# A linear-attention and mixture-of-experts kernel: three batches in flight, with four engines in program order

## The chip, the cores and the metric

The kernel runs on one core of one Trainium2 chip. Time is device time in microseconds (us) of one execution, as a median over runs; lower is better. Profiles come from one further execution, taken by the hardware profiler; its span is the time from its first to its last instruction.

The engines are named as in the profile: PE is TensorE (PEld its weight loads), DVE is VectorE, ACT is ScalarE, POOL is GpSimd, SP is SyncE, which here only issues DMA transfers. "Granted clock" is the share of full speed that PE's throttle allowed, as the profile shows it.

## The reference

There are 8 batches of 576 tokens. First comes a linear attention with 8 heads of width 64, and an RMS norm; its result, 512 wide, is the input x of a layer of 4 attention experts (head width 64), of which each token uses two.

```python
kv  = einsum('bhsd,bhse->bhde', k, v)              # 64x64 per head
out = einsum('bhsd,bhde->bhse', q, kv)
x   = out / sqrt(mean(out*out, -1) + 1e-6) * g_norm
...
logits = x @ w_gate                                # 4 experts, the best 2 kept, softmax over them
for e in range(4):
    q, k, v = x @ wq[e], x @ wk[e], x @ wv[e]
    a  = softmax(causal(q @ k.T / 8))
    ye = a @ v @ wo[e]
    result += weight_of_e_for_this_token * ye
```

## The kernel before

The tokens of a batch are cut into five blocks: four of 128 and one of 64. All eight batches pass through the same two stages and an output stage. Each stage is a Python generator: it emits instructions for one piece of work and yields a number, the weight of that piece.

**stage1(b)** (lines 191 to 314) is the linear attention. PE forms kv of each head pair (`kv_pair`, L179, 80 matmul instructions), and `kv_copy` brings it to SBUF twice, by DVE (L187) and by ACT (L188). PE transposes q block by block (`q_block`, L200, copied by DVE at L205), transposes kv (L216) and multiplies it with the gate weights (L224), so that the gate's logits come out of the same product as the attention. Then for each of the five blocks: the product p_out on PE (L243, 8 instructions), a copy o_sb by DVE (L250), the squares sq by ACT (L254), and their sum ms by DVE (L260). When all five are there, DVE computes 1/sqrt(ms) for the whole batch with an integer first guess and four Newton steps of three small operations (L271 to L281), forms the logits (L284, L290), and POOL scales the five blocks to x_tok (L296). PE transposes them (p_x, L307) and ACT copies the result to xT (L312).

**stage2(b)** (lines 317 to 495) is the expert layer. DVE and ACT compute the gate (L322 to L341). PE projects v (p_v, L347, copied by DVE to vext, L354). For each of two pairs of experts: `proj` makes q and k (L365, copied by ACT at L376); `scores` makes the causal scores in five pieces (p_sc, L393), ACT takes exp into PT (L403) and POOL masks the diagonal (L408); `pv` multiplies with v (p_O, L445), and DVE normalizes into osc (L460, L461, L465); `o_t` transposes osc (L477), copied by ACT to OT (L482). The emission order is all of p_v, then proj(0), scores(0), proj(1), scores(1), the output stage of the batch before, pv(0), o_t(0), pv(1), o_t(1).

**final(b)** (lines 497 to 508) is the output stage: p_y on PE (L501), a copy by ACT (L506) and a DMA to the result, five times.

Results of PE go through eight PSUM banks in two pools: three tiles of two banks ("big": p_proj, p_sc, p_O, p_out) and two of one bank ("small": p_kv, p_q, p_kt, p_kg, p_x, p_v, p_OT, p_y). A tile is handed to its next user when its readers are done.

The order in which work is emitted is set by `weave` (lines 519 to 531): for each piece of stage2(b) it advances stage1(b+1), the side stream, until that has reached a target share of its own weights. The side stream reaches the end of its out blocks when stage2 is at 72%, and is let on to the norm and the transposes of x when stage2 is at 92%. So in the loop over b two batches are in flight: stage2 of b and stage1 of b+1. The emitted order is not the order on the engines: the framework's planner orders each engine's instructions by readiness and emission order, with durations of its own, and then sets the semaphores. Loads (`load_qkv`) of batch b+2 are emitted at the start of iteration b; q, k and v have two sets of buffers.

Of the kernel before, what the change touches and what calls it, by code (L numbers as in the profile page):

```python
# [10 lines left out]
FP32R = mybir.dt.float32r  # L11
BF16 = mybir.dt.bfloat16
# [6 lines left out]
def kernel(  # L19
# [45 lines left out]
    def small(shape, name, dtype=FP32):  # L65
        return ps1.tile(shape, dtype, tag="small", name=name)
# [121 lines left out]
            nc.scalar.copy(kv2[pp, :, hh * Dh : (hh + 1) * Dh], p_kv[pp, :, :])  # L188


    def stage1(b, res):
        qb, kb, vb = loads[b]
        qT = s1.tile([P, NCH, S], FP32, tag="qT", name="qT", bufs=1)
        kvb, kv2 = kvx[b % 2], kv2s[b % 2]
# [39 lines left out]
            q_block(i)  # L234
            yield 0.5

        xT = s1.tile([P, NCH, S], FP32R, tag="xT", name="xT")
        lg8, ms = lg8s[b % 2], mss[b % 2]

        for i, (t0, nt) in enumerate(blocks):  # L240
# [33 lines left out]
            out=y[:].bitcast(I32), in0=half[:], scalar1=-1.0, scalar2=float(0x5F3759DF),  # L274
            op0=AluOpType.mult, op1=AluOpType.add,
        )
        for it in range(4):
            u, w, y2 = tiny("u"), tiny("w"), tiny("y")
            nc.vector.scalar_tensor_tensor(out=u[:], in0=y[:], scalar=0.5, in1=y[:], op0=AluOpType.mult, op1=AluOpType.mult)
            nc.vector.tensor_tensor(out=w[:], in0=u[:], in1=m, op=AluOpType.mult)  # L280
            nc.vector.scalar_tensor_tensor(out=y2[:], in0=w[:], scalar=1.5, in1=y[:], op0=AluOpType.subtract, op1=AluOpType.mult)  # L281
            y = y2
        gl = blk.tile([P, NB * H, E], FP32, tag="gl", name="gl")
        nc.vector.tensor_tensor(  # L284
# [9 lines left out]
        for i, (t0, nt) in enumerate(blocks):  # L294
# [5 lines left out]
                op=AluOpType.mult,  # L300
            )
            xts.append(xt)
        yield 0.0
        for i, (t0, nt) in enumerate(blocks):
            p_x = small([P, NCH, P], "p_x")
            for c in range(NCH):
# [7 lines left out]
        res["xT"] = xT  # L314


    def stage2(b, res, prev_y):
        xT = res["xT"]
        lg8 = lg8s[b % 2]
        m8 = moe.tile([P, NB, 8], FP32, tag="m8", name="m8")  # L320
# [20 lines left out]
        nc.vector.tensor_tensor(out=gate[:], in0=gt[:], in1=rden[:].unsqueeze(2).to_broadcast([P, NB, E]), op=AluOpType.mult)  # L341

        vx = vexts[b % 2]
        for i, (t0, nt) in enumerate(blocks):
            p_v = small([P, E * Hd], "p_v")
            for c in range(NCH):
                nc.tensor.matmul(  # L347
                    p_v[:nt, :],
                    lhsT=xT[:, c, t0 : t0 + nt],
                    rhs=w_r["v"][:, c, :, :].rearrange("p e f -> p (e f)"),  # L350
                    start=(c == 0),
                    stop=(c == NCH - 1),
                )
            nc.vector.tensor_copy(  # L354
                out=vx[:nt, i, :, 0:Hd], in_=p_v[:nt].rearrange("p (e f) -> p e f", e=E)
            )
            yield 0.47

        def proj(pr):
            out_t = []  # L360
# [20 lines left out]
            res["qk", pr] = out_t  # L381

        def scores(pr):
            qTp, kTp = res["qk", pr]
            PT = moe.tile([P, 2, strips], BF16, tag="PT", name="PT", bufs=3)
# [38 lines left out]
            piece([(3, 3 * P, S), (4, 4 * P, S)])  # L424
            mask(3)
            mask(4)
            yield 0.2
            res["PT", pr] = PT

        OT = moe.tile([P, EP, S], BF16, tag="OT", name="OT")  # L430

        def pv(pr):
            PT = res["PT", pr]
            p_O = big("p_O")
            inv = moe.tile([P, NB, 2], FP32, tag="inv", name="inv")
            osc = moe.tile([P, NB, 2, Hd], BF16, tag="osc", name="osc")
            groups = ((0, (0, 1, 2)), (1, (3, 4)))
            for bank, qcs in groups:
                for n, qc in enumerate(qcs):
                    s0, nq = blocks[qc]  # L440
                    for el in range(2):
                        for kb in range(qc + 1):
                            nk = blocks[kb][1]
                            col = strip_off[kb] + s0 - kb * P
                            nc.tensor.matmul(  # L445
                                p_O[:nq, bank, (2 * n + el) * (Hd + 1) : (2 * n + el + 1) * (Hd + 1)],
                                lhsT=PT[:nk, el, col : col + nq],
                                rhs=vx[:nk, kb, 2 * pr + el, :],
                                start=(kb == 0),
                                stop=(kb == qc),  # L450
                            )
                    yield 0.11 * (qc + 1)
                for sub in ((qcs,) if bank == 0 else ((3,), (4,))):
                    nq = blocks[sub[0]][1]
                    n0, nn = sub[0] - qcs[0], len(sub)
# [15 lines left out]
            res["osc", pr] = osc  # L471
# [12 lines left out]

        yield from proj(0)
        yield from scores(0)
        yield from proj(1)
        yield from scores(1)
        if prev_y is not None:
            yield from prev_y  # L490
        yield from pv(0)
        yield from o_t(0)
        yield from pv(1)
        yield from o_t(1)
        res["OT"] = OT

    def final(b, OT):
        for qc, (s0, nq) in enumerate(blocks):
            p_y = small([P, D], "p_y")
# [8 lines left out]
            yield 0.45  # L508


    W1, W2 = 14.0, 14.3
    OUT_END = 11.6 / W1

    def target(a):
        if a < 0.92:
            return min(a / 0.72, 1.0) * OUT_END
        return 1.0

    def weave(main, side):
        a = s = 0.0  # L520
        live = side is not None
        for c in main:
            a += c / W2
            while live and s < target(a):
                try:
                    s += next(side) / W1
                except StopIteration:
                    live = False
        if live:
            for _ in side:  # L530
                pass

    res = {}
    for _ in stage1(0, res):
        pass
    y_gen = None
    for b in range(B):
        if b + 2 < B:
            loads[b + 2] = load_qkv(b + 2)
        nxt = {}  # L540
        weave(stage2(b, res, y_gen), stage1(b + 1, nxt) if b + 1 < B else None)
        y_gen = final(b, res["OT"])
        res = nxt
    for _ in y_gen:
        pass


# [28 lines left out]
```

## Time and profile before

| | |
|---|---|
| three timed runs | 361.71, 362.43, 363.38 us; median 362.43 |
| profiled execution | 362.53 us, of which the span is 360.7 |
| mean granted clock of PE | 0.837 |
| PE busy | 291.8 us, 81% of the span, 2616 instructions |
| DVE busy | 188.2 us, 52%, 561 instructions |
| ACT busy | 153.0 us, 42%, 273 instructions |
| POOL busy | 80.4 us, 22%, 148 instructions |
| DMA | 30.42 MB read, 9.44 MB written |

A busy PE isn't PE at its peak: its matmuls are pipelined and their ends are modelled, so a matmul row's duration is longer than the distance to the next start. A rate is better read from the starts of successive groups in the timeline. In the timeline each row has the start, the busy time, the engine, the line, the operation with out<-in, and the count; brackets at the end hold the idle time before it and what ended that. The chain of waits follows the work that ended last back from the end; "issue" in it is time in which the engine waited for nothing that the profile shows.

### The profile page before, as it was taken

What the parts mean: (1) busy time and instruction counts of PE and PEld (TensorE: products, weight loads), DVE (VectorE), ACT (ScalarE), POOL (GpSimd) and SP (SyncE); (2) the same over time, 40 slices, a digit from 0 to 9 for tenths busy, and PEclk for the clock granted to TensorE, in tenths of its full rate; (3) what the DMA queues carried; (4) which work ended last, traced back from release to release, by engine and by line L of the source; (5) the groups of instructions that cost most, each with busy time, mean ns of one, the idle gap of its engine ahead of it and who ended that gap; (6) DMA issues with size and microseconds to landing.
All of it is one profiled execution on the core that took longest, in us unless ns stands there. A gap on an engine that the chain in (4) does not pass through costs nothing.

```text
span 360.7 us, 6721 instructions
## 1 busy us (share of the span) xinstructions
PE 291.8 (81%) x2616; PEld 234.8 (65%) x2624; DVE 188.2 (52%) x561; ACT 153.0 (42%) x273; POOL 80.4 (22%) x148
## 2 busy tenths in 40 slices
PE   2782898849994999949995899949996799949883
PEld 2581687638863788638964698638874598728551
DVE  0259654772458444781558444781458534783040
ACT  0202345432581336622572326722663326713833
POOL 8000602150220502150220502141210502132220
PEclk9997599977997599956998599966998589965966
DMA  7968999901737066600872056700002000300213
GB/s 218 214 167 222 241 266 263 207 16 45 220 89 176 2 207 135 185 0 13 250 177 87 2 159 164 195 11 2 2 37 93 2 2 0 133 1 2 88 45 132
DMA packets 75280, 40.30 MB, mean 112 GB/s; under 512 B 54000, under 2 KB 70384, under 8 KB 75248
## 3 DMA queue, kind: packets, MB, share of 16 engines
q1 hardware_dynamic: 75248, 39.86, 42.6%
q8 instruction: 21, 0.34, 0.4%
q14 instruction: 11, 0.09, 0.1%
HBM read 30.42 MB, written 9.44 MB: 110 GB/s over the span
## 4 chain that ended last, share of the span: by engine, by line
PE 56%; issue 22%; ACT 9%; POOL 5%; DVE 4%; DMA 1%; SPq 1%; DVEq 0%; ACTq 0%; POOLq 0%
PE p_proj L365 11%; PE p_x L307 10%; PE p_v L347 7%; PE p_kv L179 7%; PE p_q L200 5%; PE p_out L243 5%; ACT PT L403 4%; POOL x_tok L296 4%; PE p_sc L393 4%; PE p_kg L224 2%; PE p_y L501 2%; DVE o_sb L250 2%; DMA v_b<-in_v_dram 1%; POOL PT L408 1%; ACT y L506 1%
## 5 line engine op out<-in xcount | busy, mean ns | idle before, releaser
L307 PE MATMUL p_x<-ident_f,x_tok 128*128 128x128 f32 (+1 forms) x160 | 39.2, 411 | 39.2 <-POOL x_tok L296 38.1
L408 POOL TENSOR_SCALAR_AFFINE_SELECT PT<-PT 128x256 bf16<-128x256 bf16 (+1 forms) x80 | 29.9, 383 | 167.8 <-ACT PT L403 167.0
L296 POOL TENSOR_TENSOR x_tok<-o_sb,y 128x512 f32<-128x512 f32 (+1 forms) x40 | 42.1, 1083 | 96.7 <-DVE y L281 96.7
L403 ACT ACTIVATE PT<-p_sc 128x576 bf16<-128x576 f32 (+3 forms) x80 | 53.5, 712 | 17.7 <-PE p_sc L393 17.6
L307 PEld LDWEIGHTS p_x<-ident_f,x_tok 128*128 128x128 f32 (+1 forms) x160 | 26.9, 216 | 48.5 <-POOL x_tok L296 45.3
L243 PE MATMUL p_out<-kvx,qT 128*128 128x136 f32 (+1 forms) x320 | 45.8, 291 | 1.6 <-ACT PT L403 0.6
L243 PEld LDWEIGHTS p_out<-kvx,qT 128*128 128x128 f32 (+1 forms) x320 | 38.9, 182 | 6.3 <-ACT PT L403 3.3
L205 DVE COPY qT<-p_q 128x512 f32<-128x512 f32 (+1 forms) x40 | 24.8, 637 | 27.7 <-PE p_q L200 27.7
L354 DVE CAST vext<-p_v 128x256 bf16<-128x256 f32 (+1 forms) x40 | 17.0, 425 | 39.5 <-PE p_v L347 39.1
L254 ACT ACTIVATE sq<-p_out 128x512 f32<-128x512 f32 (+1 forms) x40 | 23.8, 595 | 27.8 <-DVE o_sb L250 19.2
L250 DVE COPY o_sb<-p_out 128x544 f32<-128x544 f32 (+1 forms) x40 | 28.8, 720 | 12.9 <-PE p_out L243 10.6
L260 DVE TENSOR_REDUCE ms<-sq 128x8 f32<-128x520 f32 (+1 forms) x40 | 27.3, 684 | 12.7 <-ACT sq L254 12.7
L445 PE MATMUL p_O<-vext,PT 128*128 128x65 bf16 (+2 forms) x480 | 29.1, 200 | 4.9 <-DVE osc L465 4.2
L179 PE MATMUL p_kv<-v_b,k_b 128*64 128x64 f32 x512 | 28.1, 275 | 6.0 <-DMA v_b<-in_v_dram 5.9
L445 PEld LDWEIGHTS <-PT 128*128 128x128 bf16 (+2 forms) x480 | 23.2, 103 | 13.8 <-issue 9.7
L179 PEld LDWEIGHTS p_kv<-v_b,k_b 128*64 128x64 f32 x512 | 25.2, 187 | 8.0 <-DMA k_b<-in_k_dram 4.5
L347 PE MATMUL p_v<-wv_r,xT 128*128 128x256 f32 (+1 forms) x160 | 30.4, 329 | 0.0
L312 ACT CAST xT<-p_x 128x512 fp32r<-128x512 f32 (+1 forms) x40 | 21.7, 543 | 18.0 <-PE p_x L307 17.9
L393 PE MATMUL p_sc<-qTp,kT 64*128 64x288 f32 (+2 forms) x192 | 25.0, 338 | 2.3 <-ACT PT L403 1.5
L347 PEld LDWEIGHTS p_v<-wv_r,xT 128*128 128x128 f32 (+1 forms) x160 | 25.0, 215 | 1.8
L365 PE MATMUL p_proj<-xT,wq_r 128*128 128x288 f32 x128 | 25.7, 321 | 0.3 <-ACT PT L403 0.3
L501 PE MATMUL p_y<-wo_b,OT 128*128 128x512 bf16 (+1 forms) x72 | 23.4, 409 | 1.8 <-ACT OT L482 1.4
(67 smaller groups left out, 370.5 us busy)
## 6 DMA issues: line engine op xcount, KB each, us to landing
q_b<-in_q_dram SPq DMA_DIRECT2D x32, 256.0 KB, 4.7
out_dram<-y SPq DMA_DIRECT2D x32, 256.0 KB, 2.0
k_b<-in_k_dram SPq DMA_DIRECT2D x7, 1024.0 KB, 5.8
v_b<-in_v_dram SPq DMA_DIRECT2D x7, 1024.0 KB, 8.6
k_b<-in_k_dram SPq DMA_DIRECT2D x4, 256.0 KB, 4.2
v_b<-in_v_dram SPq DMA_DIRECT2D x4, 256.0 KB, 4.5
k_rem<-in_k_dram SPq DMA_DIRECT2D x8, 128.0 KB, 8.5
v_rem<-in_v_dram SPq DMA_DIRECT2D x8, 128.0 KB, 7.5
```

The costliest lines, as they stand in the source:

```text
L179: nc.tensor.matmul(p_kv[hh * Dh : (hh + 1) * Dh, c, :], lhsT=lk, rhs=rv, start=(j == 0), stop=(j == NF), skip_group_check=True,)
L243: nc.tensor.matmul(p_o[:nt, c // 2, (c % 2) * 2 * GW : (c % 2 + 1) * 2 * GW], lhsT=qT[:, c, t0 : t0 + nt], rhs=kvb[:, c, :, :].rearrange(" ...
L250: nc.vector.tensor_copy(out=ob[:nt, i].rearrange("p (k h) g -> p k (h g)", k=2), in_=p_o[:nt, :, 0 : 4 * GW])
L296: nc.gpsimd.tensor_tensor(out=xt[:nt], in0=ob[:nt, i, :, 0:Dh], in1=y[:nt, i * H : (i + 1) * H].unsqueeze(2).to_broadcast([nt, H, Dh]), op ...
L307: nc.tensor.transpose(p_x[:, c, :nt], xts[i][:nt, 2 * c : 2 * c + 2, :].rearrange("p h d -> p (h d)"), ident_f[:nt, :nt],)
L347: nc.tensor.matmul(p_v[:nt, :], lhsT=xT[:, c, t0 : t0 + nt], rhs=w_r["v"][:, c, :, :].rearrange("p e f -> p (e f)"), start=(c == 0), stop= ...
L365: nc.tensor.matmul(p_p[:, s, 0:HALF], lhsT=w_r[nm][:, c, 2 * pr : 2 * pr + 2, :].rearrange("p e f -> p (e f)"), rhs=xT[:, c, s * HALF : (s ...
L393: nc.tensor.matmul(p_s[:, el, o : o + hi - lo], lhsT=kTp[pb, kb * P : (kb + 1) * P], rhs=qTp[pb, lo:hi], start=True, stop=True,)
L403: nc.scalar.activation(PT[:, :, d0 : d0 + o], p_s[:, :, 0:o], ACTF.Exp, scale=scale)
L408: nc.gpsimd.affine_select(out=d, in_=d, compare_op=AluOpType.is_ge, fill=0.0, base=0, pattern=[[0, 2], [1, w]], channel_multiplier=-1,)
L445: nc.tensor.matmul(p_O[:nq, bank, (2 * n + el) * (Hd + 1) : (2 * n + el + 1) * (Hd + 1)], lhsT=PT[:nk, el, col : col + nq], rhs=vx[:nk, kb ...
L501: nc.tensor.matmul(p_y[:nq, :], lhsT=OT[:, pr, s0 : s0 + nq], rhs=wo_b[:, pr, :], start=(pr == 0), stop=(pr == EP - 1),)
```

## The change

stage1 is cut in two. `stage_a` is stage1 up to x_tok; `stage_x` holds the five transposes p_x and their copies to xT. stage2 becomes `stage_s`. A loop iteration merges three batches: stage_s of b, stage_x of b+1 and stage_a of b+2. Before the loop, stage_a(0) runs alone, and then stage_x(0) beside stage_a(1). Each stream has a start and an end in the iteration (stage_s 0 to 1, stage_x 0.05 to 0.4, stage_a 0.1 to 1.0); `merge` always advances the stream that stands earliest.

All of it is traced under `tc.manual_schedule` with PE, ACT, DVE and POOL named: on these engines the instructions stay in the order in which they are emitted, and the planner doesn't move them. SP's DMA issues are not in the list.

Within stage_s the order is written out as a string of keys: Q0, Q1 the projections, V p_v, S0, S1 the scores, P0, P1 p_O, T0, T1 the transposes of osc, Y the output stage of the batch before. The pieces of `pv` are cut so that the normalization is emitted with the last p_O piece of its group. Loads of batch b+3 are emitted at the start of iteration b.

The norm takes three Newton steps in place of four. Each step's last operation had given (w - 1.5) * y, of the wrong sign, which four steps cancel; `reverse0=True` makes it (1.5 - w) * y.

```diff
-    def stage1(b, res):
+    def stage_a(b, res):
...
-        xT = s1.tile([P, NCH, S], FP32R, tag="xT", name="xT")
...
-        for it in range(4):
+        for it in range(3):
...
-            nc.vector.scalar_tensor_tensor(out=y2[:], in0=w[:], scalar=1.5, in1=y[:], op0=AluOpType.subtract, op1=AluOpType.mult)
+            nc.vector.scalar_tensor_tensor(
+                out=y2[:], in0=w[:], scalar=1.5, in1=y[:], op0=AluOpType.subtract, op1=AluOpType.mult, reverse0=True
+            )
...
-        yield 0.0
+        res["x_tok"] = xts
+
+
+    def stage_x(res):
+        xts = res["x_tok"]
+        xT = s1.tile([P, NCH, S], FP32R, tag="xT", name="xT")
         for i, (t0, nt) in enumerate(blocks):
             p_x = small([P, NCH, P], "p_x")
...
-    def stage2(b, res, prev_y):
+    def stage_s(b, res, prev_y):
...
-                    yield 0.11 * (qc + 1)
+                    if qc != qcs[-1]:
+                        yield 0.11 * (qc + 1)
...
+                yield 0.11 * (qcs[-1] + 1)
...
-        yield from proj(0)
-        yield from scores(0)
-        yield from proj(1)
-        yield from scores(1)
-        if prev_y is not None:
-            yield from prev_y
-        yield from pv(0)
-        yield from o_t(0)
-        yield from pv(1)
-        yield from o_t(1)
-        res["OT"] = OT
-
+        st = {"V": v_proj(), "Q0": proj(0), "Q1": proj(1), "S0": scores(0), "S1": scores(1)}
+        st.update({"P0": pv(0), "P1": pv(1), "T0": o_t(0), "T1": o_t(1), "Y": prev_y})
+        order = (
+            "Q0 Q0 V V S0 V S0 V S0 V S0 Q1 S0 Q1 S1 Y S1 Y S1 P0 P0 P0 S1 P0 P0 S1 Y T0 Y Y P1 P1 P1 P1 P1 T1"
+        )
+        for key in order.split():
+            if st[key] is not None:
+                yield next(st[key])
...
+    def merge(*streams):
+        live = [[t0, t0, (t1 - t0) / cost, gen] for gen, cost, t0, t1 in streams if gen is not None]
+        while live:
+            x = min(live, key=lambda x: x[0])
+            try:
+                x[0] += next(x[3]) * x[2]
+            except StopIteration:
+                live.remove(x)
+
+    CA, CX, CS = 11.8, 2.25, 14.5
+    with tc.manual_schedule(engines={mybir.EngineType.PE, mybir.EngineType.Activation, mybir.EngineType.DVE, mybir.EngineType.Pool}):
+        res = [dict() for _ in range(B)]
+        merge((stage_a(0, res[0]), CA, 0.0, 1.0))
+        loads[2] = load_qkv(2)
+        merge((stage_x(res[0]), CX, 0.3, 0.6), (stage_a(1, res[1]), CA, 0.0, 1.0))
+        y_gen = None
+        for b in range(B):
+            if b + 3 < B:
+                loads[b + 3] = load_qkv(b + 3)
+            merge(
+                (stage_s(b, res[b], y_gen), CS, 0.0, 1.0),
+                (stage_x(res[b + 1]) if b + 1 < B else None, CX, 0.05, 0.4),
+                (stage_a(b + 2, res[b + 2]) if b + 2 < B else None, CA, 0.1, 1.0),
+            )
+            y_gen = final(b, res[b]["OT"])
+        for _ in y_gen:
+            pass
```

More of the change, by code (lines that the diff above doesn't have):

```diff
@@ L343, in stage2, with v_proj @@
         vx = vexts[b % 2]
[L344 to L352, printed above, removed]
-                )
[L354 to L357, printed above, removed]
+        def v_proj():
+            for i, (t0, nt) in enumerate(blocks):
+                p_v = small([P, E * Hd], "p_v")
+                for c in range(NCH):
+                    nc.tensor.matmul(
+                        p_v[:nt, :],
+                        lhsT=xT[:, c, t0 : t0 + nt],
+                        rhs=w_r["v"][:, c, :, :].rearrange("p e f -> p (e f)"),
+                        start=(c == 0),
+                        stop=(c == NCH - 1),
+                    )
+                nc.vector.tensor_copy(
+                    out=vx[:nt, i, :, 0:Hd], in_=p_v[:nt].rearrange("p (e f) -> p e f", e=E)
+                )
+                yield 0.47
         def proj(pr):
-            out_t = []
+            out_t = res["qk", pr] = []
             for nm in ("q", "k"):
@@ L380, in proj @@
                 yield 1.0
-            res["qk", pr] = out_t
         def scores(pr):
             qTp, kTp = res["qk", pr]
-            PT = moe.tile([P, 2, strips], BF16, tag="PT", name="PT", bufs=3)
+            PT = res["PT", pr] = moe.tile([P, 2, strips], BF16, tag="PT", name="PT", bufs=3)
             def piece(parts):
@@ L427, in scores @@
             yield 0.2
-            res["PT", pr] = PT
-        OT = moe.tile([P, EP, S], BF16, tag="OT", name="OT")
+        OT = res["OT"] = moe.tile([P, EP, S], BF16, tag="OT", name="OT")
         def pv(pr):
@@ L435, in pv @@
             inv = moe.tile([P, NB, 2], FP32, tag="inv", name="inv")
-            osc = moe.tile([P, NB, 2, Hd], BF16, tag="osc", name="osc")
+            osc = res["osc", pr] = moe.tile([P, NB, 2, Hd], BF16, tag="osc", name="osc")
             groups = ((0, (0, 1, 2)), (1, (3, 4)))
@@ L470, in pv @@
                     )
-            res["osc", pr] = osc
+                yield 0.11 * (qcs[-1] + 1)
         def o_t(pr):
@@ L483, in o_t @@
             yield 0.5
-        yield from proj(0)
-        yield from scores(0)
-        yield from proj(1)
-        yield from scores(1)
-        if prev_y is not None:
-            yield from prev_y
-        yield from pv(0)
-        yield from o_t(0)
-        yield from pv(1)
-        yield from o_t(1)
-        res["OT"] = OT
+        st = {"V": v_proj(), "Q0": proj(0), "Q1": proj(1), "S0": scores(0), "S1": scores(1)}
[6 more added lines that the diff above has]
+                yield next(st[key])
+        for g in st.values():
+            assert g is None or next(g, None) is None
     def final(b, OT):
@@ L508, in final @@
             yield 0.45
[L511 to L545, printed above, removed]
+    def merge(*streams):
[20 more added lines that the diff above has]
+                (stage_a(b + 2, res[b + 2]) if b + 2 < B else None, CA, 0.1, 1.0),
+            )
+            y_gen = final(b, res[b]["OT"])
+        for _ in y_gen:
+            pass
 _INS = ['q', 'k', 'v', 'g_norm', 'moe_w_gate', 'moe_wq', 'moe_wk', 'moe_wv', 'moe_wo']
```

## The prediction

> **What bounds the kernel now.** I read the share of busy time first: PE 81% of the span, DVE 52%, ACT 42%. PE is the engine to look at, but it isn't full. The chain of waits, in order of time, repeats one pattern in each batch:
>
> ```profile
> 188.71 9.90 issue
> 198.65 1.19 POOL x_tok L296
> 199.88 3.17 PE p_x L307 x12
> ...
> 229.71 9.89 issue
> 239.65 1.19 POOL x_tok L296
> 240.88 3.17 PE p_x L307 x12
> ```
>
> From one first p_x to the next it is 41.00 us. The last 10 us before each are the tail of stage1 on DVE (ms, the Newton steps, y); then GpSimd scales x_tok, and only then can PE transpose it. The window table around that point (columns: length; busy time of PE, weight loads, DVE, ACT, POOL; granted clock, DMA share, GB/s) shows what it costs:
>
> ```profile
> 192.50:196.00 3.50, 1.97 (x28) 1.35 (x25) 2.79 (x17) 0.73 (x2) 0.00 (x0) 0.93 0.17 37
> 196.00:199.90 3.90, 0.02 (x1) 0.02 (x1) 3.50 (x21) 0.24 (x1) 1.25 (x2) 0.50 0.00 0
> 199.90:205.70 5.80, 5.62 (x27) 4.29 (x27) 2.69 (x6) 3.11 (x6) 3.96 (x4) 0.50 0.00 0
> 205.70:209.20 3.50, 3.50 (x46) 3.28 (x47) 0.43 (x1) 0.37 (x1) 0.00 (x0) 0.50 0.02 5
> 209.20:213.00 3.80, 3.80 (x64) 3.55 (x61) 1.70 (x4) 0.94 (x3) 0.00 (x0) 1.00 0.27 57
> ```
>
> PE stands still for 4 us, the clock falls to 0.50, and it stays there 9.3 us after work resumes. PE's work of one batch at full clock, from starts of one group to the next in the timeline at 170 to 191 us: kv 80 x 0.029 = 2.3, 20 p_v 2.7, 32 projections at 0.146 = 4.7, 20 + 20 + 4 transposes at 0.10 = 4.4, p_sc 2.8, p_kg 1.0, 40 p_out at 0.122 = 4.9, p_y 2.4, 60 p_O at 0.055 = 3.3, p_OT 0.7: **29.2 us of 41.0**. The boundary is where most of the other 12 us lie.
>
> **The change, part by part.** A batch's norm and x_tok are computed one iteration before its p_x, and four engines issue strictly in program order. That sounds as if the boundary were covered. I wrote out the order that the merge gives from its yields: an iteration starts Q0, px0, Q0, kv, px1, V, V, and ends out3, P1 x3, out4, T1, norm and x_tok. So px0 of batch b+1 is PE's second group in iteration b, and its x_tok is the last thing of iteration b-1. Only T1 and one projection lie between. I follow the period in three pieces.
>
> (1) From out0's end to px0, the chain is DVE's. In program order each out block is o_sb, then ms, and ms needs ScalarE's square, which comes after o_sb. The timeline of the first batch shows the links; and at 26.25 a second o_sb stands in the gap, which strict order forbids:
>
> ```profile
> 25.32 0.72 DVE L250 COPY o_sb<-p_out 128x544 f32<-128x544 f32 x1 [0.63 <-PE p_out L243]
> 26.08 0.60 ACT L254 ACTIVATE sq<-p_out 128x512 f32<-128x512 f32 x1 [10.25 <-DVE o_sb L250]
> 26.25 0.72 DVE L250 COPY o_sb<-p_out 128x544 f32<-128x544 f32 x1 [0.20 <-PE p_out L243]
> 26.89 0.68 DVE L260 TENSOR_REDUCE ms<-sq 128x8 f32<-128x520 f32 x1
> ```
>
> One block: 0.72 + 0.04 + 0.60 + 0.04 + 0.65 = 2.05 us of DVE, against 0.98 us of PE (8 x 0.122). Between the five blocks stand the osc groups: 1.2 (P0's last two), 1.0 and 1.2 (P1), from rows of 0.17 + 0.15 + 0.28 and 0.20 + 0.15 + 0.56 us with their gaps. Then the Newton part: before, half at 32.56 to gl at 35.81 = 3.25 for four steps; one step is three operations 0.23 apart, so three steps take 2.55. Then x_tok to p_x 1.28 (y done 198.60, p_x 199.88). Sum: 5 x 2.05 + 3.4 + 2.55 + 1.28 + 0.3 of waits for PE = **17.8**. PE has 10 us of work in that stretch and waits: 1.1 before T0 (its osc stands behind out0's ms), 2.5 before T1, 4.2 before px0. Today out4's end (191.0) to px0 (199.88) is 8.9 us with 4.4 of PE work inside; afterwards 8.4 us with 1.7 inside. The dropped Newton step is thus worth its 0.7 us, and the stall is longer.
>
> (2) From px0 to the end of kv: px0 0.4, Q0 1.17, kv 2.35 = 3.9 at full clock. The clock: today it fell at 196.0 though PE was busy 1.97 of the 3.5 us before; the new order leaves 1.7 busy of 8.4, so I take it as fallen. Today it came back about 3.5 us after projections, p_v and kv ran without gaps (205.7 to 209.2). Here these follow px0 at once, so 5.2 us of half clock (bounds 3.5 and 7, one and two such stretches), of which half is lost: **6.5**. This is where the change gains: today 9.3 us are at half clock, and p_x goes at GpSimd's pace. If the clock did not fall it would be 3.9.
>
> [...]
>
> (3) From kv's end to out0's end. V.0 needs the PSUM buffer of kv (two small ones). Its copies alternate between DVE and ScalarE:
>
> ```profile
> 128.59 0.42 DVE L187 COPY kvx<-p_kv 64x256 f32<-64x256 f32 x1 [3.10 <-PE p_kv L179]
> 129.04 0.36 ACT L188 COPY kv<-p_kv 64x256 f32<-64x256 f32 x1 [4.99 <-DVE kvx L187]
> ...
> 129.71 0.43 DVE L187 COPY kvx<-p_kv 64x256 f32<-64x256 f32 x1
> ...
> 130.17 0.37 ACT L188 COPY kv<-p_kv 64x256 f32<-64x256 f32 x1 [0.77 <-DVE kvx L187]
> ```
>
> kv ended at 128.48; the last copy ends 2.06 later (1.9 without the cast between). Today p_v and projections run in that time; in program order V.0 waits, with only px1 (0.4) before it. Then PE has p_v 2.7, three p_x 1.2, S0 1.5, Q1 2.3, q_blocks 2.0, kt 0.45, kg 1.0, four S1 1.1, two p_y 1.1, P0 1.1, out0 1.0 = 15.4. I add 1.0 for waits on copies that program order no longer fills (xT before V.1 and V.4, kT before S1, kvT before kg, y before q3; each 0.1 to 0.3). Sum 1.9 + 15.4 + 1.0 = **18.3**. The gate chain of DVE (4.3 us, 198.60 to the end of gate) now stands before kvx; it ends 3.0 after px0, before kv does, so it costs nothing while kv ends later than that.
>
> Period: 17.8 + 6.5 + 18.3 = **42.6 us, against 41.0**. Bounds for the unseen terms: waits in (3) 0 to 2.5, clock 3.9 to 7.3, DVE's gaps in (1) from 14.5 (no wait for the square) to 19.
>
> **The ends of the program.** Before, the first p_x of batch 1 is at 77.45. After, batch 1's first stage follows batch 0's at once: five out blocks from 25.3 end at 35.6, Newton 38.1. kv of batch 1 meanwhile, cold and waiting for its loads (k_rem and v_rem issued 33.4 and 34.1, landing 3.9 to 8.6 later): done about 41.5; copies 43.4, kt to q4 5.5, first out block ready 49, five blocks 59.2, Newton and x_tok 63. So px0 at **63** (60 to 70). Six periods follow, the first 1 shorter (no Y). At the other end, two iterations have no first stage. Before, the last 31.5 us (329.2 to 360.7) held one attention batch, two output stages and little else. After px0 of batch 7 I count 5.6 to V.0, 8.6 to the end of Q1, 0.8 for kT and 11 to T1 (26 in all, ScalarE busy 17 of it), 21 for the last batch without p_x, and 8.5 from T1 to the end, as now (351.8 to 360.7): **55.5**. Before, px0 of batch 7 to the end was 37.9. What the start gains (14.5), the end loses (17.6).
>
> Sum: 63 + 6 x 42.6 - 1 + 55.5 = 373.1, plus the 1.8 us that lie around the profiled span (362.53 against 360.7): **375 us**. The profiled execution stands 0.1 above the median of 362.43.
>
> **Loads.** The load of batch b+3 is issued in iteration b, when the same buffers come free as today (two sets); DMA share is 0.44 of a batch, so I cost it at nothing. If a load were late, kv would wait, up to the 8.6 us of a landing, once.
>
> **Rivals.**
> A (faster): DVE's chain is shorter than I sum, so that px0's wait falls under 2 us and the clock holds. Needed: 2.2 us of the 17.8. It exists if ms seldom waits (5 x 0.66 = 3.3); for it: today all waits of ms for the square are 12.7 us over 40, 0.3 each. Against: today's 0.3 comes from operations put between, as at 26.25. Period 42.6 - 2.2 - 2.6 = 37.8, total 63 + 226.8 - 1 + 54 + 2 = 345. 0.20, 338 to 356.
> B: the stall stays but the clock doesn't fall: 40.0, 375 - 6 x 2.6 = 359. Against it, the row at 196.0. 0.09.
> C (slower): the three large PSUM buffers go round in order, so S1's fourth piece gets that of P0, which is free only after osc, 3.5 us after out0 and not 0.5; out1's block starts 1.9 later: 44.5, 375 + 6 x 1.9 = 386. 0.16.
> D: what stands ahead of the ordered part (wo_b, which needs wo_st, issued 39.96 and 5.3 us to land) is kept ahead on DVE too: the first copies move from 12.8 to 46, over 400. 0.05.
> That the order isn't as written is covered by A.
>
> **How the numbers follow.** Forecast 0.50, 363 to 385. The range holds 8 in 10 from half of A to C: 350 to 390. A measurement tells 0.5% (1.8 us) from no change. Faster: A and most of B, 0.27; same 0.06; slower 0.67.
>
> **What would show it.** Right: the first p_x of consecutive batches 42 to 43 us apart; PE idle 3 to 5 us before each px0, released by x_tok; clock 0.50 around it but for 4 to 6 us of work; ms waiting some 0.6 us for sq in all 40; V waiting for ACT kv; an end of 55 us. Wrong: a period below 40 or a clock that holds; a wait of S1 for osc would be C.

## The result and the profile after

The changed kernel takes **393.36 us** (four runs, 392.47 to 397.87) against 362.07 (360.21 to 363.38) of the kernel before in the same session: ratio 1.089, 95% interval 1.080 to 1.099, slower by 31 us. The forecast was 375, with a range up to 390. The profiled execution took 392.68 us with a span of 390.8. Medians and ratios below leave out executions more than 1.5% above the kernel's fastest: of the kernels tried one each of e1 and e9, and two of e3's four (328.7 and 330.3 us; with them e3's median is 326.5).

The busy shares of the profile after, in the form of the small table above:

```profile
PE 296.2 (76%) x2624; PEld 235.7 (60%) x2624; DVE 191.0 (49%) x537; ACT 156.0 (40%) x273; POOL 79.8 (20%) x148
```

No engine has more to do worth naming (PE +4.4 us, the other three within 3), and the mean granted clock even rose, 0.837 to 0.888. So the 30 us of span are mostly waits: PE's idle time grew by 25.7 us. The chain of waits (start, us, what) has the old pattern, on one batch after another:

```profile
180.20 16.25 issue
196.49 1.19 POOL x_tok L297
197.72 1.11 PE p_x L313 x4
```

It is the boundary of before, with 16.25 us of "issue" in place of 9.9 (15 to 16 before the first p_x of each of the batches 3 to 7): x_tok still ends last, and p_x still waits for it, though x_tok belongs to the iteration before. After the first period it is now 44 to 46 us from one first p_x to the next, not 41.0. The window table of one iteration (length; busy time of PE, weight loads, DVE, ACT, POOL; clock, DMA share, GB/s), cut at the prediction's three pieces and, from 183.73 on, where the clock changes:

```profile
152.56:158.20 5.64, 5.64 (x93) 5.30 (x93) 2.82 (x6) 1.89 (x4) 3.99 (x4) 0.70 0.00 0
158.20:160.05 1.85, 0.66 (x9) 0.42 (x5) 0.84 (x2) 0.77 (x3) 0.00 (x0) 1.00 0.24 59
160.05:177.50 17.45, 16.64 (x135) 12.95 (x135) 6.83 (x15) 10.52 (x17) 3.09 (x8) 1.00 0.61 176
177.50:183.73 6.23, 5.71 (x49) 4.09 (x50) 4.41 (x11) 3.30 (x7) 0.64 (x2) 1.00 0.84 190
183.73:187.14 3.41, 1.15 (x14) 1.03 (x14) 2.14 (x5) 1.54 (x3) 0.00 (x0) 1.00 0.37 115
187.14:193.97 6.83, 6.03 (x38) 5.06 (x38) 3.30 (x11) 1.11 (x2) 0.00 (x0) 0.50 0.00 0
193.97:197.38 3.41, 0.37 (x3) 0.14 (x1) 3.00 (x17) 0.00 (x0) 0.89 (x1) 1.00 0.00 0
197.38:200.80 3.42, 3.08 (x14) 2.81 (x16) 3.11 (x9) 1.34 (x4) 3.42 (x5) 0.50 0.01 2
```

Up to 183.73 PE is nearly full, but for 1.2 us of the second row. Then it stands still twice, at 184.9 and at 194.3, and in each stop the clock halves (at 187.14 and 197.38). The first stop was not forecast. The timeline shows it (start, busy us, engine, line, operation, in brackets the idle time before and its releaser):

```profile
186.29 0.69 DVE L259 TENSOR_REDUCE ms<-sq 128x8 f32<-128x520 f32 x1 [0.72 <-ACT sq L253]
...
187.32 0.56 DVE L472 TENSOR_TENSOR osc<-p_O,inv 128x384 bf16<-128x384 f32 x1
187.94 1.69 PE L451 MATMUL p_O<-vext,PT 128*128 128x65 bf16 x18 [3.06 <-DVE osc L472]
...
189.67 0.17 DVE L467 RECIPROCAL inv<-p_O 128x2 f32<-128x2 f32 x1 [1.78 <-PE p_O L451]
...
191.74 0.72 DVE L249 COPY o_sb<-p_out 64x544 f32<-64x544 f32 x1 [0.81 <-PE p_out L242]
```

PE's second p_O group writes the same PSUM tile (its other bank) from which DVE still has to normalize the first group. That osc stands in DVE's order behind ms of an out block, and ms waits for ScalarE's square. So PE waits 3.06 us for DVE; then, at half clock, DVE waits 1.78 and 0.81 us for PE. The wait doesn't need the half clock: in the iteration before it is as long, and there the clock is still full until 146.17:

```profile
144.14 1.18 PE L451 MATMUL p_O<-vext,PT 128*128 128x65 bf16 x18 [3.06 <-DVE osc L472]
...
145.36 0.17 DVE L467 RECIPROCAL inv<-p_O 128x2 f32<-128x2 f32 x1 [1.27 <-PE p_O L451]
```

DVE then waits only 1.27 us. Over the program, PE's waits and that of ms read:

```profile
PE p_x L313 <- POOL x_tok L297: 31.0, 8, 7.3
DVE ms L259 <- ACT sq L253: 27.9, 39, 1.0
PE p_O L451 <- DVE osc L472: 24.5, 16, 3.1
```

(us in all, times, longest.) Before, the same three were 38.1, 12.7 and 4.2.

### The profile page after: what moved, and what is told of

It is laid out like the page before. It is cut to its first block, busy times and chain, and to the rows that moved or that the text cites. A ratio compares the mean times of both kernels' runs of the same rounds, so it can differ in the third digit from the quotient of the medians.

```text
span 390.8 us, 6711 instructions
## 1 busy us (share of the span) xinstructions
PE 296.2 (76%) x2624; PEld 235.7 (60%) x2624; DVE 191.0 (49%) x537; ACT 156.0 (40%) x273; POOL 79.8 (20%) x148
## 4 chain that ended last, share of the span: by engine, by line
PE 46%; issue 29%; DVE 12%; ACT 5%; POOL 4%; DMA 1%; SPq 1%; ACTq 0%; DVEq 0%; POOLq 0%
PE p_proj L373 9%; PE p_v L355 6%; PE p_sc L400 6%; PE p_kv L179 5%; PE p_x L313 5%; PE p_q L200 4%; POOL x_tok L297 3%; PE p_y L506 3%; PE p_O L451 3%; DVE o_sb L249 3%; DVE osc L472 2%; PE p_out L242 2%; PE p_kg L224 2%; ACT sq L253 2%; DMA v_b<-in_v_dram 1%
## 5 line engine op out<-in xcount | busy, mean ns | idle before, releaser
L297 POOL TENSOR_TENSOR x_tok<-o_sb,y 128x512 f32<-128x512 f32 (+1 forms) x40 | 41.6, 1069 | 145.3 <-DVE y L280 145.3
L410 ACT ACTIVATE PT<-p_sc 128x576 bf16<-128x576 f32 (+3 forms) x80 | 56.2, 708 | 19.3 <-PE p_sc L400 17.7
L313 PE MATMUL p_x<-ident_f,x_tok 128*128 128x128 f32 (+1 forms) x160 | 28.9, 311 | 31.3 <-POOL x_tok L297 31.0
L242 PE MATMUL p_out<-kvx,qT 128*128 128x136 f32 (+1 forms) x320 | 49.4, 305 | 1.3 <-ACT sq L253 1.3
L451 PE MATMUL p_O<-vext,PT 128*128 128x65 bf16 (+2 forms) x480 | 30.9, 201 | 24.5 <-DVE osc L472 24.5
L242 PEld LDWEIGHTS p_out<-kvx,qT 128*128 128x128 f32 (+1 forms) x320 | 42.7, 192 | 5.3 <-ACT sq L253 3.9
L313 PEld LDWEIGHTS p_x<-ident_f,x_tok 128*128 128x128 f32 (+1 forms) x160 | 19.0, 159 | 38.1 <-POOL x_tok L297 33.4
L259 DVE TENSOR_REDUCE ms<-sq 128x8 f32<-128x520 f32 (+1 forms) x40 | 27.7, 693 | 27.9 <-ACT sq L253 27.9
L205 DVE COPY qT<-p_q 128x512 f32<-128x512 f32 (+1 forms) x40 | 25.2, 634 | 25.7 <-PE p_q L200 25.7
L400 PE MATMUL p_sc<-qTp,kT 64*128 64x288 f32 (+2 forms) x192 | 34.9, 370 | 1.5 <-ACT kT L384 1.5
L249 DVE COPY o_sb<-p_out 128x544 f32<-128x544 f32 (+1 forms) x40 | 28.6, 715 | 10.8 <-PE p_out L242 10.8
L355 PE MATMUL p_v<-wv_r,xT 128*128 128x256 f32 (+1 forms) x160 | 28.1, 304 | 7.2 <-ACT kv L188 7.2
L362 DVE CAST vext<-p_v 128x256 bf16<-128x256 f32 (+1 forms) x40 | 17.0, 425 | 33.6 <-PE p_v L355 33.6
L179 PEld LDWEIGHTS p_kv<-v_b,k_b 128*64 128x64 f32 x512 | 23.7, 178 | 11.9 <-DMA k_b<-in_k_dram 4.6
L355 PEld LDWEIGHTS p_v<-wv_r,xT 128*128 128x128 f32 (+1 forms) x160 | 20.8, 181 | 12.3 <-ACT kv L188 8.6
L373 PE MATMUL p_proj<-xT,wk_r 128*128 128x288 f32 x128 | 28.0, 377 | 0.0
```

The costliest lines, as they stand in the source:

```text
L179: nc.tensor.matmul(p_kv[hh * Dh : (hh + 1) * Dh, c, :], lhsT=lk, rhs=rv, start=(j == 0), stop=(j == NF), skip_group_check=True,)
L242: nc.tensor.matmul(p_o[:nt, c // 2, (c % 2) * 2 * GW : (c % 2 + 1) * 2 * GW], lhsT=qT[:, c, t0 : t0 + nt], rhs=kvb[:, c, :, :].rearrange(" ...
L249: nc.vector.tensor_copy(out=ob[:nt, i].rearrange("p (k h) g -> p k (h g)", k=2), in_=p_o[:nt, :, 0 : 4 * GW])
L297: nc.gpsimd.tensor_tensor(out=xt[:nt], in0=ob[:nt, i, :, 0:Dh], in1=y[:nt, i * H : (i + 1) * H].unsqueeze(2).to_broadcast([nt, H, Dh]), op ...
L313: nc.tensor.transpose(p_x[:, c, :nt], xts[i][:nt, 2 * c : 2 * c + 2, :].rearrange("p h d -> p (h d)"), ident_f[:nt, :nt],)
L355: nc.tensor.matmul(p_v[:nt, :], lhsT=xT[:, c, t0 : t0 + nt], rhs=w_r["v"][:, c, :, :].rearrange("p e f -> p (e f)"), start=(c == 0), stop= ...
```

## The experiments

**Theories.** Mine after the result: strict program order makes DVE's waits for squares into everybody's waits, and the whole loss lies between the out blocks and the next p_x. Rivals: the three-batch plan itself is worse; one engine's order alone is at fault; the p_x are merely emitted too early. All ratios are to the kernel before, in the same session.

| kernel | us | ratio (95%) |
|---|---|---|
| after | 393.4 | 1.089 (1.080 to 1.099) |
| e2: DVE not held in order | 376.7 | 1.042 (1.038 to 1.046) |
| e5: PE not held | 371.8 | 1.029 (1.025 to 1.032) |
| e6: ScalarE not held | 400.4 | 1.109 (1.103 to 1.115) |
| e9: PE and DVE not held | 341.5 | 0.941 (0.934 to 0.948) |
| e3: no engine held | 324.0 | 0.894 (0.891 to 0.898) |
| e11: e3 and the split of e7 | 323.7 | 0.894 (0.887 to 0.901) |
| e4: before, with three Newton steps | 348.8 | 0.963 (0.959 to 0.967) |
| e1: late p_x | 403.9 | 1.116 (1.112 to 1.120) |
| e13: e1, gate chain later | 379.1 | 1.055 (1.044 to 1.066) |
| e7: second p_O group in its own PSUM tile | 374.9 | 1.037 (1.033 to 1.042) |
| e8: ms one block later | 385.1 | 1.064 (1.060 to 1.068) |
| e12: e7 and e8 | 362.2 | 1.000 (0.997 to 1.003) |
| e14: e12, emission reordered | 337.3 | 0.935 (0.928 to 0.943) |
| e15: e14's emission, no engine held | 309.1 | 0.857 (0.849 to 0.865) |

### Which engine's order costs? (e2, e5, e6, e9, e3)

Only the list of engines differs; e3 has `if True:` in the place of the `with`. An engine that isn't in the list has its order set by the planner, as in the kernel before.

```diff
-    with tc.manual_schedule(engines={mybir.EngineType.PE, mybir.EngineType.Activation, mybir.EngineType.DVE, mybir.EngineType.Pool}):
+    with tc.manual_schedule(engines={mybir.EngineType.PE, mybir.EngineType.Activation, mybir.EngineType.Pool}):
```

e2, DVE:

> DVE is taken out of the list of engines in program order, so the planner may put other operations between o_sb and ms. If DVE's strict order is what makes the chain from out0 to x_tok 20 us long: the wait of ms for sq falls from 28 us to about 13, the osc of P1's first three blocks no longer waits behind out3, the chain is 3 to 5 us shorter in each iteration, total 362 to 375. If PE's order alone decides: within 1% of 393.

Measured 376.7: 16.7 less than after, a little above the range. The wait of ms fell from 27.9 to 10.3 us, that of p_O for osc only to 17.0.

e5, PE:

> PE is taken out of the list of engines in program order; DVE, ACT and POOL stay in it. Theory (PE stands behind one late operand at a time: px0, V.0, P1's fourth block; each has ready work behind it): most of the 67 us between the version without any order (326.5) and the change (393.4) come back, 335 to 360; PE's waits for x_tok, kv and osc fall to a third. Rival (DVE's order makes x_tok late and nothing on PE can hide that): like the version with DVE free, 370 to 385.

Measured 371.8: the rival's range. p_x still waits 36.5 us for x_tok and ms 28.1 for sq; PE's freedom doesn't shorten DVE's chain. What went away is PE's wait of p_O for osc, from 24.5 to 2.2 us, close to the 21.6 us gained.

e6, ScalarE:

> ACT is taken out of the list; PE, DVE and POOL stay in it. ACT's own waits are for operands that PE and DVE deliver in order anyway: 388 to 394. If ACT's order costs by itself (exp of the gate, which waits for DVE, ahead of the copies of q, and the squares behind the exps): below 380.

Measured 400.4, worse than after and outside both expectations. With the planner's order for ScalarE ms waits 33.6 us (27.9 in after) and p_O for osc 28.6 (24.5). Why the planner chose that order I didn't follow up.

e9, PE and DVE:

> PE and DVE are taken out of the list, ACT and POOL stay in program order. With PE alone free the time was 371.8, with DVE alone free 376.7, with none held 326.5. Theory (each of the two orders holds the other: a free DVE waits for an ordered PE and the other way round): with both free nearly all comes back, 326 to 340. If the two gains only add, or ACT's order holds them: 393 - 21.6 - 16.7 = 355.

Measured 341.5, just above the first range. The two together gain 51.9 us, singly 21.6 and 16.7: they hold each other, and the gains more than add. Another 17.5 us stand between this and e3, so freeing ScalarE and GpSimd as well gains too, though ScalarE alone lost 7.

e3, none:

> The same three-batch emission and order string, with no engine held in program order: the planner orders all four as it did before the change. If strict order is what costs, and the three-batch pipeline by itself is harmless: 358 to 368 (a period of about 40 with three Newton steps, and an end that is 10 to 18 us longer against a start that is 10 to 14 us shorter). If the three-batch merge itself costs (the end, px0 right behind the norm): 375 to 395.

Measured 324.0, far below both ranges. Program order costs 69 us here, and the three-batch plan itself is good. Its PE timeline at a boundary shows what the planner does otherwise:

```profile
192.81 1.14 PE L242 MATMUL p_out<-kvx,qT 128*64 128x136 f32 x8
194.27 1.32 PE L373 MATMUL p_proj<-xT,wq_r 128*128 128x288 f32 x8 [0.32 <-ACT sq L253]
196.33 0.68 PE L373 MATMUL p_proj<-xT,wk_r 128*128 128x288 f32 x3 [0.73 <-ACT qTp L384]
196.85 1.19 PE L451 MATMUL p_O<-vext,PT 128*128 128x65 bf16 x18
...
201.48 0.41 PE L400 MATMUL p_sc<-qTp,kT 64*128 64x320 f32 x2 [0.87 <-ACT PT L410]
201.96 1.07 PE L313 MATMUL p_x<-ident_f,x_tok 128*128 128x128 f32 x4
```

It runs the last p_out first, then one projection of the next iteration and the start of the second, and only then the second p_O group (18 instructions, now without a wait for osc); scores follow, and p_x comes when x_tok is there. Both stops of PE are filled, but for waits under 1 us on ScalarE: p_x waits 3.9 us for x_tok in the whole program, not 31.0, and p_O never waits for osc.

### What is a Newton step worth? (e4)

```diff
-        for it in range(4):
+        for it in range(3):
...
-            nc.vector.scalar_tensor_tensor(out=y2[:], in0=w[:], scalar=1.5, in1=y[:], op0=AluOpType.subtract, op1=AluOpType.mult)
+            nc.vector.scalar_tensor_tensor(out=y2[:], in0=w[:], scalar=1.5, in1=y[:], op0=AluOpType.subtract, op1=AluOpType.mult, reverse0=True)
```

> The kernel before with three Newton steps for four, and nothing else. The Newton part stands in the chain of waits of each of the 8 batches, 0.70 us a step: 5.6 us less, 356 to 358. If the chain only seemed to bind there: within 1 us of 362.

Measured 348.8: 13.2 us less than before (11.9 to 14.7), not the 5.6 of eight times 0.7. The window tables, cut where the clock changes, of before:

```profile
154.57:168.23 13.66, 9.20 (x72) 7.64 (x73) 7.02 (x31) 4.12 (x8) 5.21 (x5) 0.50 0.00 0
168.23:195.53 27.30, 25.96 (x260) 20.91 (x259) 15.79 (x39) 14.77 (x26) 3.73 (x10) 1.00 0.66 174
```

and of e4:

```profile
148.61:162.26 13.65, 9.78 (x80) 8.10 (x82) 6.14 (x31) 4.11 (x8) 5.21 (x5) 0.50 0.00 0
162.26:189.57 27.31, 25.80 (x254) 20.71 (x251) 16.01 (x41) 14.90 (x27) 3.73 (x10) 1.00 0.65 174
189.57:196.40 6.83, 3.39 (x16) 2.65 (x16) 4.63 (x25) 2.00 (x5) 4.62 (x5) 0.50 0.00 0
196.40:227.12 30.72, 29.29 (x312) 23.76 (x311) 16.51 (x39) 16.63 (x30) 4.32 (x11) 1.00 0.57 155
```

Every stretch is a whole number of 3.413 us: 4 and 8 of them before, over and over; 4, 8, 2 and 9 in e4. Before, the period of 41.0 is just 12 units, so each boundary meets the clock's changes at the same place and has four units at half clock. With 0.7 us less it meets them at changing places, and the half-clock phase is now four units, now two; the four periods from 114 to 272 us change with it: 38.1 us with a phase of two units, 40.5 and 40.8 with one of four. On average it is 1.7 us less per period, of which the step itself is 0.7.

### Are the p_x merely too early? (e1, e10, e13)

e1 moves stage_x later in the iteration:

```diff
-                (stage_x(res[b + 1]) if b + 1 < B else None, CX, 0.05, 0.4),
+                (stage_x(res[b + 1]) if b + 1 < B else None, CX, 0.3, 0.65),
```

> The five p_x move from 0.05-0.4 of the iteration to 0.3-0.65; nothing else. My theory (PE stands before px0 because x_tok is the last thing of the iteration before, and DVE's program order sets when it is ready): the wait of p_x for x_tok falls from 31 us in all to under 5, but the wait moves to V.0, because the kv copies stand on DVE behind the same norm and the gate chain (4.3 us): V.0 starts about 11 us after out4's end and not 13.6. Period 42 to 43, total 378 to 385. Rival (only the place of p_x in PE's order is wrong): the 4.3 us before px0 and the half clock after it go, period 38 to 39, total 355 to 362.

Measured 403.9: slower, and both expectations missed. e10 is the same kernel again, for its profile:

> The same kernel as the one with the p_x at 0.3-0.65 (404.7 us, where 378 to 385 was expected), once more for a profile. My reading: the wait has moved from px0 to V.0 as foreseen, but the five p_x and their copies now stand in the stretch in which ACT does the exps, and the clock falls for longer: p_v waits for ACT's kv copies over 4 us in each iteration, and PE is at half clock over 8 us an iteration. If p_v doesn't wait there, the loss is elsewhere.

It took 411.25 us in its one execution, 1.8% above e1's median. The first of PE's waits:

```profile
PE p_v L355 <- ACT kv L188: 30.1, 6, 6.7
```

The reading held: p_v waits 5.0 us a time, and a period has five units of 3.41 us at half clock. The wait for x_tok is gone, as meant (31.0 to 1.3), but another of the same size takes its place: p_v waits for the kv copies (7.2 in after). On DVE those copies stand behind the gate chain, which stands behind the norm. DVE's chain had been hidden behind p_x's own wait, and now it ends last on the next instruction that needs DVE. e13 tests this: as e1, but with the gate chain emitted behind the first two p_v ("G" in the string), so that kv is copied first.

```diff
-            "Q0 Q0 V V S0 V S0 V S0 V S0 Q1 S0 Q1 S1 Y S1 Y S1 P0 P0 P0 S1 P0 P0 S1 Y T0 Y Y P1 P1 P1 P1 P1 T1"
+            "Q0 Q0 V V G S0 V S0 V S0 V S0 Q1 S0 Q1 S1 Y S1 Y S1 P0 P0 P0 S1 P0 P0 S1 Y T0 Y Y P1 P1 P1 P1 P1 T1"
```

> The version with the p_x at 0.3-0.65 (404.7 us), and the gate chain of stage_s (4.3 us of DVE) emitted behind the first two p_v in place of ahead of everything. If V.0 waited there for kv copies that stand on DVE behind norm and gate: the copies come 3.5 us earlier in each of six iterations and the half clock shrinks by one window or two, 370 to 385, and p_v's wait for ACT kv falls from 30 to under 12 us. If the p_x themselves are in the way in the stretch of the exps: 395 or more.

Measured 379.1, within the range and 25 us under e1; p_v's wait is 11.3 us. It is also 14 us under after: late p_x do help, once the gate chain no longer stands ahead of the kv copies.

### The shared PSUM tile, and ms (e7, e8, e12, e11)

e7 gives the second p_O group a one-bank tile of the small pool:

```diff
+                p_b = p_O[:, 0, :] if bank == 0 else small([P, 4 * (Hd + 1)], "p_O1")
...
-                                p_O[:nq, bank, (2 * n + el) * (Hd + 1) : (2 * n + el + 1) * (Hd + 1)],
+                                p_b[:nq, (2 * n + el) * (Hd + 1) : (2 * n + el + 1) * (Hd + 1)],
```

> The second group of p_O blocks gets a PSUM tile of its own (one of the small ones), where it had the second bank of the tile that the first group is read from. All four engines in program order. Theory: PE's wait of 24.5 us for osc before the fourth block goes, P1's last blocks and out4 come 2.5 us earlier in each of six iterations, the chain from out0 to px0 is 17.8 and not 20.2 us: 374 to 381. Rival (DVE is the bound there, PE only waits with it): within 3 us of 393.

Measured 374.9, within the range: 18.5 us less. p_O no longer waits for osc (24.5 in after), ms still waits 27.9. This one dependency was the first stop of PE. Its timeline now shows PE's waits where the prediction had them, ahead of T1 and of px0:

```profile
182.08 1.36 PE L452 MATMUL p_O<-vext,PT 128*128 128x65 bf16 x24
...
185.49 0.34 PE L485 MATMUL p_OT<-ident_b,osc 128*128 128x128 bf16 x3 [0.98 <-DVE osc L473]
...
192.50 1.12 PE L313 MATMUL p_x<-ident_f,x_tok 128*128 128x128 f32 x4 [4.39 <-POOL x_tok L297]
```

e8 emits ms of a block behind o_sb of the next, so that DVE no longer waits for the square:

```diff
+            if i > 0:
+                reduce(i - 1)
...
-            nc.vector.tensor_reduce(ms[:nt, i, :], sq[:nt], axis=AX_X, op=AluOpType.add)
+            if i == NB - 1:
+                reduce(i)
```

> On DVE, ms of an out block is emitted behind o_sb of the next block, so that DVE no longer stands still for the square. All four engines in program order. Theory (five blocks of 2.05 us in the chain from out0 to px0): the wait of ms for sq falls from 27.9 to about 6 us, 0.65 us in four blocks of each iteration, 2.6 x 7: 374 to 378. If PE's wait for osc sets that stretch as well, half of it or less: 382 to 390.

Measured 385.1, 8.2 less: the second range. The waits of ms fell from 27.9 to 0.4 us, but little of that is worth time while p_O still waits 18.8 us for osc. So my theory, that DVE's waits for squares are the loss, doesn't hold by itself.

e12 does both:

> Both repairs with all four engines in program order: p_O's second group in its own tile (alone 374.9, 18.5 less) and ms behind the next o_sb (alone 385.1, 8.3 less). Theory (with PE's wait for osc gone, the whole 2.6 us of the skew comes out of the chain from out0 to px0): 393.4 - 18.5 - 6.8 x 2.6 = 357, range 354 to 362; if the two gains overlap: 366 to 373.

Measured 362.2, just above the range; 31.1 less than after, where the two alone add to 26.7. The period is 41 us again, and the time that of before. p_x still waits 32.8 us for x_tok.

e11 puts the split into e3:

> No engine held in program order, and the second group of p_O in a PSUM tile of its own. If PE's wait for osc before the fourth p_O block is still paid there: 2 to 8 us less, 318 to 324. If the planner already puts other work there: within 2 us of 326.5, or worse by the small PSUM tile that it takes from p_x and p_v.

Measured 323.7 (321.8 to 326.2), within the noise of e3's 324.0. By the numbers as put it falls into the first range, but those are reckoned from 326.5 for e3. The trace of e3 decides: p_O waits for osc nowhere in it, so there was nothing for the split to gain.

### A better order by hand (e14, e15)

e14 takes e12 and moves three things: T1 behind the next iteration's projections ("U"), the gate chain behind the fourth p_v, and stage_a to 0.0 to 0.85 of the iteration, so that norm and x_tok end before it does; stage_x starts at 0.09.

```diff
-            "Q0 Q0 V V S0 V S0 V S0 V S0 Q1 S0 Q1 S1 Y S1 Y S1 P0 P0 P0 S1 P0 P0 S1 Y T0 Y Y P1 P1 P1 P1 P1 T1"
+            "Q0 Q0 U V V S0 V S0 V S0 V G S0 Q1 S0 Q1 S1 Y S1 Y S1 P0 P0 P0 S1 P0 P0 S1 Y T0 Y Y P1 P1 P1 P1 P1"
...
-                (stage_x(res[b + 1]) if b + 1 < B else None, CX, 0.05, 0.4),
-                (stage_a(b + 2, res[b + 2]) if b + 2 < B else None, CA, 0.1, 1.0),
+                (stage_x(res[b + 1]) if b + 1 < B else None, CX, 0.09, 0.4),
+                (stage_a(b + 2, res[b + 2]) if b + 2 < B else None, CA, 0.0, 0.85),
```

> All four engines in program order, as in the change, with another order: p_O's second group in its own tile, ms behind the next o_sb, stage_a at 0 to 0.85 of the iteration and not 0.1 to 1.0 (norm and x_tok ahead of P1's blocks), T1 moved behind the two projections of the next iteration, the gate behind the fourth p_v. Theory (strict order costs only through what stands right behind norm, osc and kv copies): nothing waits over 1.5 us on PE, no half clock in the middle, period 32 to 34, total 305 to 325. Rival (strict order itself costs, whatever stands where, since it can't adapt to the durations): 340 to 360.

Measured 337.3, between the ranges: 56 us less than after with all four engines still in program order. p_x waits 4.1 us for x_tok in all (32.8 in e12); what is left are mostly waits on copies, the longest of a kind 0.3 to 0.9 us, and in each period still 3.41 or 6.83 us at half clock. Which of the moves gains how much was not tried one by one.

e15 is e14's emission without the `with`:

> The emission of the reordered version, with no engine held in program order. If the planner's gain over strict order was only that the first order was bad: the same as the reordered version within 3%. If the planner's order is better whatever is emitted: 315 to 325 and clearly below the reordered one.

Measured 309.1, below both: 14.3% under before and the fastest of all. One period of its middle in the window table:

```profile
193.70:226.90 33.20, 32.19 (x332) 25.96 (x330) 22.26 (x67) 18.70 (x34) 8.84 (x15) 1.00 0.11 37
```

PE is busy 32.2 of 33.2 us, at full clock throughout; in the same view e14 has a period of 37.3 and a clock of 0.95. Even the better order by hand costs 28 us against the planner's.

## Why the prediction was right in its sign and wrong in its size

| term, us | predicted | measured |
|---|---|---|
| start to px0 of batch 1 | 63 | 67.3 |
| the first period | 41.6 | 40.9 |
| the next five | 213.0 | 224.9 |
| px0 of batch 7 to the end | 55.5 | 57.7 |
| span | 373.1 | 390.8 |

**Right.** The order read from the yields, and what follows from it: px0 waits for x_tok (3.4 us at 197.72, 4.2 forecast), ms waits about 0.7 us for sq in 39 of 40 blocks, V.0 starts 1.85 us behind kv's end, waiting for the kv copies (1.9), the clock halves around px0. Piece (2), px0 to the end of kv, took 5.6 us (6.5), piece (3) 19.3 (18.3); that these two misses cancel is luck.

**The step that failed** is "0.3 of waits for PE" in the sum for piece (1). The piece took 20.2 us where 17.8 was forecast, and DVE waited 1.78 + 0.81 = 2.6 us for PE in it. I had taken PE's p_O blocks as running whenever they were next, with PE's wait of 2.5 us behind them, before T1, where it costs DVE nothing. But the second p_O group needs the first one's osc, so PE's wait stands ahead of it (3.06 us, and none before T1), and DVE then waits for p_O and out4 in its turn: 1.27 us at full clock, 2.6 where the clock has halved. It could be read from the trace of before, in a row that I passed over:

```profile
PE p_O L445 <- DVE osc L465: 4.2, 7, 0.7
```

There no wait was longer than 0.7 us; in program order p_O can't move. P0's two groups have the same dependency, 0.78 us at 176.07, inside piece (3). e7 shows the step: without the dependency out0's end to px0 takes 17.5 us (175.03 to 192.50), the next five periods 210.0 (213.0 forecast, 224.9 measured). Its whole gain, 18.5 us, is a little more than the 17.7 by which the forecast span missed; that is in part chance, since e7's start is still 3.4 us later than forecast and its end 1.7 shorter.

**The clock.** I took 5.2 us of half clock per period in one stretch. In the period shown there were 10.2, in two (187.14 and 197.38), the first behind the stop that I had not forecast; the other periods differ. The row at 192.5, from which I took the fall, was cut across the clock's own steps, with the fall, at 195.53, inside it. Cut at the steps, the stretch before the fall had PE busy 68%, not 56 (1.97 of 3.50 us):

```profile
192.11:195.53 3.42, 2.32 (x33) 1.65 (x30) 2.48 (x15) 0.59 (x1) 0.00 (x0) 1.00 0.26 58
```

That the clock can fall behind a stretch with work in it stays right: PE was busy 2.32 of 3.42 us there, and in after 1.15 of 3.41 before the fall at 187.14. But the busy share alone doesn't decide it: in after, the clock held behind this stretch, with PE busy 52%, and was full until 234.92:

```profile
228.09:231.51 3.42, 1.79 (x22) 1.44 (x21) 2.04 (x4) 1.82 (x4) 0.00 (x0) 1.00 0.38 113
```

**The ends.** 4.2 us at the start: batch 0's five p_x, 4.3 us by their rows there, lie between batch 1's q and kv transposes, and my count of that stretch left them out. The first out block was ready at 53.2, not 49; kv ended at 41.66 against 41.5. The 2.2 us at the other end weren't broken down.

**The Newton step** "is thus worth its 0.7 us": as a piece of the chain, yes; in the kernel before, e4 shows 1.7 us a period, for its half-clock phases change by whole units of 3.413 us.

**"Costs nothing while kv ends later"**, of the gate chain, held in the kernel after. e1 took that cover away, and p_v then waited up to 6.7 us.

**Rivals.** A (ms seldom waits) didn't occur, and its price was wrong: e8 takes these waits away in program order and reaches 385.1, not 345. e3 has 7.9 us of them and takes 324.0, but there the rest of the order differs as well. The 2 us of wait under which A had the clock hold were an estimate of mine, and no run isolated such a limit. B didn't occur. C asked the right question of the wrong buffer: S1's fourth piece ran without a wait at 178.18, and PE waited for osc inside p_O's own tile instead. D didn't occur; wo_b ran at 49.91 and held up nothing.

**What stays open.** e3 gains more than e7 and e8 explain; which further moves of the planner carry it was not tried one by one. e6's loss isn't explained. And what makes the clock fall wasn't isolated: the two rows above speak against a fixed share of busy time.

## What to carry to other kernels

A wider pipeline and a fixed order are two changes, to be tried apart: here the plan gained 25 us on the two-batch kernel with the same Newton steps (348.8 to 324.0), and the order took 69 back. Before engines are put in program order, write down for each the next instruction that it waits for and what stands ahead of that on the other engine, with two regions of one PSUM tile counted as one dependency, as p_O's two banks were here (24.5 us of waits for osc in after, none in e7); where two engines wait for each other in turn, the waits add up (3.06 us of PE at 187.94, then 1.78 and 0.81 of DVE). And taking one wait away showed the next: e1 moved 30 us from x_tok to the kv copies.

## What the runs showed of the hardware

**The clock changed on a grid of 3.413 us.** In before, after, e4, e7 and e14 the changes lie whole multiples of 3.413 us apart, as the window tables of before and of e4 show (13.66, 27.30, 6.83, 30.72). The half clock at a stop lasted whole units as well: one (197.38), two (187.14) or four (before). It came behind a stretch with work in it too: the clock fell at 187.14 after PE had been busy 1.15 of 3.41 us, as the row at 183.73 shows. Some periods came out near a whole number of units: 41.0 us in before are 12, 40.9 to 41.3 in e12's later periods as well, 47.8 to 48.1 in e10's middle ones are 14. Why they do so in these kernels and not in after (44.0 to 46.3 us) was not looked into.

**VectorE beside GpSimd.** The two 128x20 tensor_tensor operations sh and mk of the gate chain change places. Before:

```profile
199.91 0.96 DVE L329 TENSOR_TENSOR sh<-lg,m 128x20 f32<-128x20 f32 x1
200.79 0.17 DVE L333 TENSOR_TENSOR mk<-lg,m 128x20 f32<-128x20 f32 x1
```

After:

```profile
197.61 0.18 DVE L335 TENSOR_TENSOR sh<-lg,m 128x20 f32<-128x20 f32 x1
197.71 1.03 DVE L339 TENSOR_TENSOR mk<-lg,m 128x20 f32<-128x20 f32 x1
```

The slow one lies under an x_tok of POOL and ends just behind it: in after, POOL's second x_tok runs from 197.63 to 198.70, and mk ends at 198.73; in before, one runs from 199.79 to 200.83, and sh ends at 200.87. In after's last batch no x_tok runs beside the chain (the last one ends at 337.09), and there mk, at 358.79, took 0.17 us, against 1.02 or 1.03 in the other seven. Whether the x_tok is what makes the operation slow, no run here isolated.
